# Gated mix of attention and SwiGLU: three instead of five of every eight score tiles are split between VectorE and ScalarE, in another order of scores, steps and late exponentials

## The chip, the core and the metric

The kernel runs on one core of a Trainium2 chip. A core has a matrix engine (TensorE, PE in the profile, with its weight loads on a row of their own, PEld), VectorE (DVE), ScalarE (ACT), GpSimd (POOL) and SyncE (SP), which issues the DMAs. The engines run side by side, each works through its own instructions in order, and they wait for one another by semaphores. Matrix products land in PSUM, a small memory of banks that hold 128x512 float32 values each; everything else lies in SBUF. The metric is the device time of one execution in microseconds (us), as the median of several.

## The reference

The input `x` has 2048 rows of 512. Attention with 32 heads of width 16 that share one key and one value head, a SwiGLU layer with an inner width of 1792, and a sigmoid gate per row that mixes the two:

```python
q = (x @ wq).reshape(B, S, H, Dh).transpose(0, 2, 1, 3)
k, v = x @ wk, x @ wv
scores = jnp.einsum("bhqd,bkd->bhqk", q, k) * (Dh ** -0.5)
o = jnp.einsum("bhqk,bkd->bhqd", softmax(scores), v)
a = o.transpose(0, 2, 1, 3).reshape(B, S, H * Dh) @ wo
b = (silu(x @ w_gate) * (x @ w_up)) @ w_down
g = sigmoid((x * gate_w).sum(-1, keepdims=True))
return g * a + (1 - g) * b
```

## The kernel before

**The units of attention.** Work is cut into units u = 16 h + kt: head h and one of 16 key tiles of 128 keys. A unit has two score tiles, each for 128 keys and 1024 queries. `score` (line 658) fills one score tile `pss` with two matmuls, one for each PSUM bank of 512 queries; there are only two such tiles (`ps_s`, two buffers of two banks), so a score can start only when the score before the last has been read out of PSUM. An exponential (`exps`, line 666) goes to `pt` in SBUF. `mix` (line 678) multiplies the unit's `pt` with the values into `po`. The softmax is not shifted by a maximum; a flag asks at the end whether that was safe.

**Two ways to empty a score tile.** A whole tile (kind "A") is read by one ScalarE instruction over 1024 columns. A split tile (kind "H") is read by two engines side by side: VectorE copies columns 512 to 1023 to `pt` as they are (line 662), ScalarE takes the exponential of columns 0 to 511 from PSUM ("d" in the table `EXPS`), and later, in place in SBUF, that of the copied half ("s", a late exponential). A split tile is out of PSUM sooner and costs VectorE a copy.

**The steps of the feed-forward layer.** Its products (gate, up, down) and the query projections are jobs of 12 or 15 steps. Every step is done in two halves of 64 rows: one job does its lower half while an earlier job does its upper half, so a step is a pair of matmuls at line 175 on different rows of PE. A job has a PSUM tile `pf` (three buffers), which VectorE empties: a copy for gate (line 265), a product with silu for up (line 292, or 294), a scaled sum for down (lines 327 and 329). A finished job gives its `pf` free only when that has run. The silu needs a tanh on ScalarE (line 274) and a VectorE instruction on two SBUF operands (line 282); the result is then cast and split (lines 106 and 107). GpSimd splits the weights (lines 106 and 107 on POOL).

**The block.** The order in the long stage is written out by hand. From unit 32 on, a block of four units has eight scores, 16 steps and the `mix` of four units. The table `STEPS` says in which order scores (S) and steps (F) are issued to PE, `KINDS` which score tiles are split, and `EXPS` in which order ScalarE does the exponentials: "3d" is the one that frees tile 3, "2s" the late one of tile 2. An entry is issued as soon as its score has been issued; those behind "|" come after all scores and after the tanh instructions that wait in `ACTS`. The scores run two units ahead: block k issues the scores of units 4k+2 to 4k+5 and mixes units 4k to 4k+3, so the first two units mixed have their `pt` from the block before. There are 118 full blocks of this kind. Behind the scores, VectorE gets up to 3.2 (`BUDGET`) of work that was put off: two entries of `LATER` (the division by the softmax sum, lines 687, 690, 696), then `DEFER` (silu, cast). When a job ends on a step that is followed within two steps by the score of a split tile, its evacuation is held back behind that score's copy (`HOLD`). The copy of a finished head's `po` (line 695) is issued once a number of scores of the block have been issued.

Of the kernel before, what the change touches and what calls it, by code (L numbers as in the profile page):

```python
# [50 lines left out]
STOP = 2  # L51
EARLY = 6
OUTS = (1, 2, 3, 0)
STEPS = "SSFFFFSFFSFFSFFFSFFFSFFS"
KINDS = "HHHAHHAA"
EXPS = ("0d", "1d", "0s", "2d", "3d", "4d", "1s", "5d", "6d", "7d", "2s", "|", "4s", "5s")
TURN = "SS" + "SFF" * 8
BUDGET = 3.2
AHEAD = 6
# [3 lines left out]
def tile_gated_mix(ctx, tc, x, wq, wk, wv, wo, w_gate, w_up, w_down, gate_w, out):  # L63
# [60 lines left out]
    def run(queue, n):  # L124
        for _ in range(min(n, len(queue))):
            queue.pop(0)()
# [508 lines left out]
    with tc.tile_pool(name="bpool", bufs=2) as bp:  # L635
# [15 lines left out]
        def score(u, j, half=False):  # L651
            h, kt = divmod(u, NT)
            if j == 0:
                new_pt(u)
            ps = ps_s.tile([P, 2 * CH], F32, name="pss")
            for b in range(2):
                rows = slice(b * RT, (b + 1) * RT)
                nc.tensor.matmul(ps[:, b * CH:(b + 1) * CH], ks[rows, kt * P:(kt + 1) * P], QS[h][rows, j, :],  # L658
                                 start=True, stop=True)
            halves.clock += 1  # L660
            pt = PT[u][:, j * 2 * CH:(j + 1) * 2 * CH]
            other = nc.vector.tensor_copy(pt[:, CH:], ps[:, CH:]) if half else None  # L662
            return pt, ps, other

        def exps(pt, ps, other=None, w=slice(None)):
            ins = nc.scalar.activation(pt[:, w], ps[:, w], AF.Exp, scale=SCALE)  # L666
            if other is not None:
                tc.declare_no_dep(getattr(ins, "ins", ins), getattr(other, "ins", other), reason="another bank")

        def mix(u):  # L670
            h, kt = divmod(u, NT)
            pt = PT.pop(u)
            if kt == 0:
                run(COPY, 1)
                PO[:] = [ps_o.tile([P, CH], F32, name="po")]
            po = PO[0]
            for c in range(NCH):
                nc.tensor.matmul(po[c * 2 * DH:(c + 1) * 2 * DH, :], vaug[:, kt, :], pt[:, c * CH:(c + 1) * CH],  # L678
                                 start=(kt == 0), stop=(kt == NT - 1))
            if kt == NT - 1:  # L680

                osb = hp.tile([P, CH], F32, name="osb")
                rsb = hp.tile([P, CH], F32, name="rsb", bufs=1)

                def invert(i):
                    w = slice(i * P, (i + 1) * P)
                    nc.vector.reciprocal(rsb[:, w], rsb[:, w])  # L687

                def store():
                    nc.vector.tensor_tensor(osb, osb, rsb, ALU.mult)  # L690
                    for c in range(NCH):
                        nc.sync.dma_start(o_d[h * DH:(h + 1) * DH, c * CH:(c + 1) * CH],
                                          osb[c * 2 * DH:c * 2 * DH + DH, :])

                COPY.append(lambda: nc.vector.tensor_copy(osb, po))
                LATER.extend([(0.8, lambda: nc.vector.stream_shuffle(rsb, osb, [DH] * 2 * DH))] +
                             [(1.0, lambda i=i: invert(i)) for i in range(TC)] + [(0.8, store)])
# [5 lines left out]
        def feed(k, more=True):  # L703
            for _ in range(k):
                if JOBS and more or halves.busy():
                    halves.step(more)

        def block(k, first, last, steps, kinds, order):
            more = k < NB - STOP
            tiles = [(u, j) for u in range(first, last) for j in range(2)]  # L710
            order = list(order)
            made = []

            def emit():
                while order and order[0] != "|" and int(order[0][0]) < len(made):
                    i, how = int(order[0][0]), order.pop(0)[1]
                    pt, ps, other = made[i]
                    if how == "s":
                        exps(pt, pt, w=slice(CH, None))
                    else:  # L720
                        exps(pt, ps, other, slice(0, CH) if kinds[i] == "H" else slice(None))

            for i, what in enumerate(steps):
                if what == "F":
                    if "S" in steps[i + 1:i + 3] and kinds[len(made):len(made) + 1] == "H":
                        HOLD.append(i)
                    feed(1, more)
                    HOLD.clear()
                elif len(made) < len(tiles):
                    made.append(score(*tiles[len(made)], kinds[len(made)] == "H"))  # L730
                    emit()
                    run(EVAC, len(EVAC))
                if len(made) > 3:
                    run(COPY, 1)
            if order:
                order.pop(0)
            run(ACTS, len(ACTS))
            emit()
            assert not order and len(made) == len(tiles)
            left = BUDGET  # L740
            for queue, n in ((LATER, 2), (DEFER, len(DEFER))):
                while n and queue and queue[0][0] <= left:
                    cost, f = queue.pop(0)
                    left, n = left - cost, n - 1
                    f()
            for u in range(BLOCK * k, BLOCK * (k + 1)):
                mix(u)
            halves.clock += 2 * LONG
# [7 lines left out]
        with tc.manual_schedule():  # L756
# [25 lines left out]
            for k in range(2 * BEGIN // BLOCK, NB):  # L782
                u = BLOCK * k
                if k == 2 * BEGIN // BLOCK:
                    n = u + 6 - (u + 1)
                    block(k, u + 1, u + 6, TURN, "A" * 2 * n, [f"{i}d" for i in range(2 * n)])
                elif k == NB - 1:
                    block(k, u + 2, u + 4, STEPS, "AAAA", ("0d", "1d", "2d", "3d", "|"))
                else:
                    block(k, u + 2, u + 6, STEPS, KINDS, EXPS)  # L790
                h = u // NT
                if k % (NT // BLOCK) == 0 and 0 < h < H - 1:
                    load_head(h + 1)
                if k == NB - EARLY:
                    load_o(OUTS[0], range(KD - 1))
# [119 lines left out]
```

## Time and profile before

| | us |
|---|---|
| median of 3 runs | 1374.03 (1373.33 to 1375.18) |
| the profiled execution's own time | 1375.01 |
| its span from first to last instruction | 1373.2 |
| PE busy in the span | 1344.7 |
| ScalarE busy | 1082.0 |
| VectorE busy | 866.1 |
| GpSimd busy | 391.1 |
| mean granted TensorE clock | 0.996 of full |

The span is cut by stage: until about 130 us come projections and a first stage of attention in which all tiles are whole, from about 140 to 1290 us the 118 blocks, and behind them the rest of the down products and the output projection. A row of a timeline has the start, the duration, the engine, the line, the operation, what is written and read, how many of a kind in sequence were merged (x4), and in brackets how long the engine was idle before and who ended that. Matmul durations overlap: on PE the distance from one start to the next is what counts.

### The profile page before, as it was taken

The numbers are of one execution on the slowest core, as the hardware profiler recorded it, in microseconds if no ns is written. First come the engines' busy times: TensorE is split into PE (matmuls) and PEld (weight loads), VectorE is DVE, ScalarE is ACT, GpSimd is POOL, SyncE is SP. The second block draws the span as 40 slices with busy tenths as digits, with TensorE's granted clock in tenths as the row PEclk, the third lists the DMA queues.
The fourth block names the chain that finished last, engine by engine and source line by source line (L and its number), as shares of the span: only waits on it lengthen the run. The fifth ranks groups of instructions, "written<-read, shape, count | busy, mean of one in ns | idle before, by whom it ended". The sixth has DMA issues, their size and how long they took to land. (4 is left out here: it accounts for less than half of the span.)

```text
span 1373.2 us, 27579 instructions
## 1 busy us (share of the span) xinstructions
PE 1344.7 (98%) x10755; PEld 798.9 (58%) x10755; DVE 866.1 (63%) x1458; ACT 1082.0 (79%) x1699; POOL 391.1 (28%) x408
## 2 busy tenths in 40 slices
PE   9999999999999999999999999999999999999998
PEld 7654565565655555655555565556555555655576
DVE  5554677577666666666576676667576676666532
ACT  4578898888888888888888888888888888888500
POOL 5140321052131242132131241232131331233344
PEclk9999999999999999999999999999999999999999
DMA  7455311131241231121241230131221221222154
GB/s 271 139 177 188 88 35 36 29 100 43 55 123 44 74 82 35 47 74 44 58 120 43 66 92 26 47 89 36 59 68 33 89 66 35 62 68 58 36 165 140
DMA packets 101495, 107.84 MB, mean 79 GB/s; under 512 B 9968, under 2 KB 69616, under 8 KB 99696
## 3 DMA queue, kind: packets, MB, share of 16 engines
q1 hardware_dynamic: 99632, 105.81, 26.8%
q8 instruction: 89, 1.46, 0.5%
q10 hardware_dynamic: 1728, 0.20, 0.1%
q14 instruction: 46, 0.38, 0.1%
HBM read 76.09 MB, written 29.36 MB: 77 GB/s over the span
## 5 line engine op out<-in xcount | busy, mean ns | idle before, releaser
L666 ACT ACTIVATE pt<-pss 128x512 f32<-128x512 f32 (+1 forms) x1024 | 753.9, 778 | 185.2 <-PE pss L658 166.5
L662 DVE COPY pt<-pss 128x512 f32<-128x512 f32 x590 | 395.4, 688 | 312.2 <-PE pss L658 295.9
L678 PE MATMUL po<-pt,vaug 128*32 128x512 f32 x4096 | 469.3, 597 | 0.0
L658 PE MATMUL pss<-qs,ks 64*128 64x512 f32 x2048 | 432.7, 418 | 5.9 <-DVE pt L662 4.0
L666 ACT ACTIVATE pt<-pt 128x512 f32<-128x512 f32 x590 | 351.8, 630 | 1.4 <-DVE pt L662 1.3
L658 PEld LDWEIGHTS pss<-qs,ks 64*128 64x128 f32 x2048 | 202.6, 184 | 197.4 <-issue 106.0
L678 PEld LDWEIGHTS po<-pt,vaug 128*32 128x32 f32 x4096 | 119.5, 110 | 272.1 <-issue 272.1
L175 PE MATMUL pf<-xh,wgh 64*128 64x512 f32 (+1 forms) x444 | 167.5, 394 | 5.0 <-DVE ht L292 4.4
L175 PE MATMUL pf<-xh,wuh 64*128 64x512 f32 (+1 forms) x440 | 167.2, 393 | 2.9 <-DVE sign L401 0.7
L175 PE MATMUL pf<-xl,wgh 64*128 64x512 f32 (+1 forms) x444 | 169.7, 390 | 0.0
L175 PE MATMUL pf<-xh,wgl 64*128 64x512 f32 (+1 forms) x444 | 169.3, 395 | 0.0
L175 PE MATMUL pf<-xh,wul 64*128 64x512 f32 (+1 forms) x440 | 167.2, 394 | 0.0
L175 PE MATMUL pf<-xl,wuh 64*128 64x512 f32 (+1 forms) x440 | 163.0, 390 | 0.0
L175 PE MATMUL pf<-wdl,hh 64*128 64x512 f32 (+1 forms) x427 | 158.2, 392 | 2.4 <-POOL wdl L107 2.4
L175 PE MATMUL pf<-wdh,hh 64*128 64x512 f32 (+1 forms) x427 | 157.5, 394 | 2.9 <-DVE ht L292 2.4
L106 POOL CAST wgh<-wraw 128x512 fp32r<-128x512 f32 x56 | 35.5, 633 | 432.3 <-PE pf L175 338.8
L175 PE MATMUL pf<-wdh,hl 64*128 64x512 f32 (+1 forms) x427 | 156.9, 392 | 0.0
L687 DVE RECIPROCAL rsb<-rsb 128x128 f32<-128x128 f32 x128 | 116.9, 934 | 3.1 <-issue 1.1
L106 POOL CAST wuh<-wraw 128x512 fp32r<-128x512 f32 x56 | 35.7, 638 | 259.8 <-PE pf L175 223.6
L175 PEld LDWEIGHTS pf<-xh,wgh 64*128 64x128 f32 (+1 forms) x444 | 81.2, 185 | 16.4 <-issue 6.4
L175 PEld LDWEIGHTS pf<-xh,wuh 64*128 64x128 f32 (+1 forms) x440 | 80.9, 184 | 12.8 <-issue 7.2
L175 PEld LDWEIGHTS pf<-wdh,hh 64*128 64x128 f32 (+1 forms) x427 | 79.0, 186 | 12.7 <-DVE ht L292 4.5
(157 smaller groups left out, 1590.7 us busy)
## 6 DMA issues: line engine op xcount, KB each, us to landing
wraw<-in_B_w_gate_dram SPq DMA_DIRECT2D x56, 256.0 KB
wraw<-in_B_w_up_dram SPq DMA_DIRECT2D x56, 256.0 KB
wraw<-in_B_w_down_dram SPq DMA_DIRECT2D x56, 256.0 KB
qs<-q_d SPq DMA_DIRECT2D x62, 192.0 KB
q_d<-hl SPq DMA_DIRECT2D x18, 256.0 KB
q_d<-hh SPq DMA_DIRECT2D x18, 256.0 KB
o_d<-osb SPq DMA_DIRECT2D x128, 32.0 KB
a_d<-acc SPq DMA_DIRECT2D x4, 1024.0 KB
```

The source lines that it names most:

```text
L106: eng_hi.tensor_copy(hi, src)
L175: ins = nc.tensor.matmul(self.ps, a, b, start=(i == 0 and not half), stop=(last and half != 0))
L658: nc.tensor.matmul(ps[:, b * CH:(b + 1) * CH], ks[rows, kt * P:(kt + 1) * P], QS[h][rows, j, :], start=True, stop=True)
L662: other = nc.vector.tensor_copy(pt[:, CH:], ps[:, CH:]) if half else None
L666: ins = nc.scalar.activation(pt[:, w], ps[:, w], AF.Exp, scale=SCALE)
L678: nc.tensor.matmul(po[c * 2 * DH:(c + 1) * 2 * DH, :], vaug[:, kt, :], pt[:, c * CH:(c + 1) * CH], start=(kt == 0), stop=(kt == NT - 1))
L687: nc.vector.reciprocal(rsb[:, w], rsb[:, w])
```

## The change

Three tables and one number:

```diff
-STEPS = "SSFFFFSFFSFFSFFFSFFFSFFS"
-KINDS = "HHHAHHAA"
-EXPS = ("0d", "1d", "0s", "2d", "3d", "4d", "1s", "5d", "6d", "7d", "2s", "|", "4s", "5s")
+STEPS = "SSFFFFFSFSFFFSFFSFFFFFSS"
+KINDS = "AHHAHAAA"
+EXPS = ("0d", "1d", "2d", "3d", "4d", "5d", "1s", "4s", "2s", "6d", "7d", "|")
...
-                if len(made) > 3:
+                if len(made) > 4:
                     run(COPY, 1)
```

In a block of the kernel before, tiles 0, 1, 2, 4 and 5 are split, and 3, 6 and 7 are whole. Now tiles 1, 2 and 4 are split, and 0, 3, 5, 6 and 7 are whole: two copies less on VectorE, and in place of two half exponentials twice one whole. PE still has eight scores, 16 steps and one mix in a block, in another order. The late exponentials of tiles 1, 4 and 2 stand together between 5d and 6d, and none is left behind "|", so that the tanh comes last. The copy of a head's `po` comes after the fifth score, not the fourth.

ScalarE, one block (between two others, without a tanh in it). Each row is an exponential; `pt<-pss` with 128x512 is the half of a split tile, with 128x1024 a whole tile, and `pt<-pt` a late one. Before:

```order
L666 ACTIVATE pt_4846<-pss_4847 128x512
L666 ACTIVATE pt_4846<-pss_4852 128x512
L666 ACTIVATE pt_4846<-pt_4846 128x512
L666 ACTIVATE pt_4868<-pss_4869 128x512
L666 ACTIVATE pt_4868<-pss_4878 128x1024
L666 ACTIVATE pt_4886<-pss_4887 128x512
L666 ACTIVATE pt_4846<-pt_4846 128x512
L666 ACTIVATE pt_4886<-pss_4909 128x512
L666 ACTIVATE pt_4921<-pss_4922 128x1024
L666 ACTIVATE pt_4921<-pss_4931 128x1024
L666 ACTIVATE pt_4868<-pt_4868 128x512
L666 ACTIVATE pt_4886<-pt_4886 128x512 x2
```

Now:

```order
L666 ACTIVATE pt_5269<-pss_5270 128x1024
L666 ACTIVATE pt_5269<-pss_5274 128x512
L666 ACTIVATE pt_5290<-pss_5291 128x512
L666 ACTIVATE pt_5290<-pss_5299 128x1024
L666 ACTIVATE pt_5309<-pss_5310 128x512
L666 ACTIVATE pt_5309<-pss_5319 128x1024
L666 ACTIVATE pt_5269<-pt_5269 128x512
L666 ACTIVATE pt_5309<-pt_5309 128x512
L666 ACTIVATE pt_5290<-pt_5290 128x512
L666 ACTIVATE pt_5350<-pss_5351 128x1024
L666 ACTIVATE pt_5350<-pss_5355 128x1024
```

The block opens with a whole tile, no late exponential stands among the first six, and three of them stand ahead of the last two whole tiles.

PE, from a block's first two scores to its third. Before (eight matmuls, four steps of down jobs):

```order
L658 MATMUL pss<-qs,ks 128x512 x4
L175 MATMUL pf<-wdl,hh 128x512
L175 MATMUL pf<-wdh,hl 128x512 x2
L175 MATMUL pf<-wdh,hh 128x512 x2
L175 MATMUL pf<-wdl,hh 128x512 x2
L175 MATMUL pf<-wdh,hl 128x512
L658 MATMUL pss<-qs,ks 128x512 x2
```

Now ten matmuls, five steps:

```order
L658 MATMUL pss<-qs,ks 128x512 x4
L175 MATMUL pf<-wdh,hl 128x512
L175 MATMUL pf<-wdl,hh 128x512
L175 MATMUL pf<-wdh,hh 128x512
L175 MATMUL pf<-wdh,hl 128x512
L175 MATMUL pf<-wdl,hh 128x512
L175 MATMUL pf<-wdh,hh 128x512
L175 MATMUL pf<-wdh,hl 128x512
L175 MATMUL pf<-wdl,hh 128x512
L175 MATMUL pf<-wdh,hh 128x512
L175 MATMUL pf<-wdh,hl 128x512
L658 MATMUL pss<-qs,ks 128x512 x2
```

The third score stands one step later, the fourth follows after one step instead of two, and the last two scores now stand side by side ahead of the mix.

VectorE, a block in which an up job ends before its silu has run, so that silu and product stand among the copies (the MEMSET is a marker that the lower half of a job has ended). Before:

```order
L662 COPY pt_7363<-pss_7364 128x512
L662 COPY pt_7363<-pss_7369 128x512
L662 COPY pt_7383<-pss_7384 128x512
L282 SCALAR_TENSOR_TENSOR ht_7307<-ht_7307,hs_7305 128x512
L292 TENSOR_TENSOR ht_7307<-ht_7307,pf_7175 128x512
L662 COPY pt_7411<-pss_7412 128x512
L401 MEMSET sign_84 1x1
L662 COPY pt_7411<-pss_7425 128x512
```

Now, in such a block:

```order
L662 COPY pt_9375<-pss_9380 128x512
L401 MEMSET sign_84 1x1
L662 COPY pt_9397<-pss_9398 128x512
L662 COPY pt_9415<-pss_9416 128x512
L282 SCALAR_TENSOR_TENSOR ht_9328<-ht_9328,hs_9326 128x512
L292 TENSOR_TENSOR ht_9328<-ht_9328,pf_9207 128x512
L401 MEMSET sign_84 1x1
```

Two copies stood behind the silu and its product; none stands there now. A silu directly followed by its product stands at 14 places before and at 13 now. The program still has 1024 score tiles; the copies go from 590 to 354.

## The prediction

> **What bounds the kernel now.** I read the page's head first, then the busy times of the long stage, then the timeline of single blocks, and last the waits of PE.
>
> ```profile
> span 1373.2 us, 27579 instructions
> PE 1344.7 (98%) x10755; PEld 798.9 (58%) x10755; DVE 866.1 (63%) x1458; ACT 1082.0 (79%) x1699; POOL 391.1 (28%) x408
> ```
>
> ```profile
> 200.00:1200.00 1000.00, 987.69 (x8258) 572.97 (x8256) 663.06 (x1122) 863.47 (x1392) 262.17 (x271) 1.00 0.23 61
> ```
>
> The second fence is the stretch from 200 to 1200 us: PE 988 of 1000, VectorE 663, ScalarE 863, the clock full. PE is the bound, but "busy" hides waits of less than a matmul's modelled length, so I measure blocks. These are the starts of the first and the last mix in that stretch, and the group that says how many matmuls of the mix lie in it:
>
> ```profile
> 204.94 3.64 PE L678 MATMUL po<-pt,vaug 128*32 128x512 f32 x32
> ...
> 1191.44 3.64 PE L678 MATMUL po<-pt,vaug 128*32 128x512 f32 x32
> ```
>
> ```profile
> L678 PE MATMUL po<-pt,vaug 128*32 128x512 f32 x3296 | 375.0, 595 | 0.0
> ```
>
> 3296 matmuls at 32 a block are 103 mixes, so 102 blocks took 986.5 us: 9.67 us each. An undisturbed block looks like this on PE:
>
> ```profile
> 815.52 3.64 PE L678 MATMUL po<-pt,vaug 128*32 128x512 f32 x32
> 819.09 0.74 PE L658 MATMUL pss<-qs,ks 64*128 64x512 f32 x4
> 819.66 0.39 PE L175 MATMUL pf<-xh,wgl 64*128 64x512 f32 x1
> ...
> 820.12 0.39 PE L175 MATMUL pf<-xl,wgh 64*128 64x512 f32 x1
> ...
> 820.35 0.39 PE L175 MATMUL pf<-xh,wgl 64*128 64x512 f32 x1
> ...
> 820.57 0.49 PE L658 MATMUL pss<-qs,ks 64*128 64x512 f32 x2
> 820.87 0.38 PE L175 MATMUL pf<-xh,wuh 64*128 64x512 f32 x1
> ...
> 821.33 0.43 PE L658 MATMUL pss<-qs,ks 64*128 64x512 f32 x2
> ...
> 822.00 0.48 PE L658 MATMUL pss<-qs,ks 64*128 64x512 f32 x2
> ...
> 822.94 0.47 PE L658 MATMUL pss<-qs,ks 64*128 64x512 f32 x2
> ...
> 824.61 0.43 PE L658 MATMUL pss<-qs,ks 64*128 64x512 f32 x2
> 824.97 3.64 PE L678 MATMUL po<-pt,vaug 128*32 128x512 f32 x32
> ```
>
> It takes 9.45 us: 3.57 from mix to first score, 5.88 for scores and steps. A step or a score costs 0.23 (820.12 to 820.35), the first two scores together 0.57 (819.09 to 819.66), and a score that had to wait for its tile 0.30 up to the next step (820.57 to 820.87). The mean of 9.67 is 0.22 above this block; over 118 blocks that is 26 us, about all that an easier VectorE or GpSimd could give back. Who made PE wait, from 160 to 1285 us, first on PE, then on its weight loads:
>
> ```profile
> PE pf L175 <- DVE ht L292: 6.8, 8, 1.6
> PE pss L658 <- DVE pt L662: 4.0, 7, 1.6
> PE pf L175 <- DVE acc L329: 1.0, 3, 0.4
> PE pf L175 <- DVE hs L265: 1.0, 4, 0.4
> ```
>
> ```profile
> PEld pss L658 <- ACT pt L666: 38.6, 171, 2.0
> ...
> PEld pf L175 <- DVE ht L292: 4.5, 6, 1.8
> ...
> PEld pf L175 <- DVE hs L265: 1.2, 2, 0.7
> ```
>
> VectorE's six rows are 18.5 us. The 38.6 us of weight loads that waited for an exponential are mostly their head start on the matmul and can't be added to the span; they say that a score's tile comes free only just in time, 171 times. The chain that ended last reaches back only to the output projection at 1359 us, so it says nothing of this stage.
>
> **The change part by part.** The sum is made against the profiled execution: 1375.01 us, 1.8 more than its span and 1.0 above the median of 1374.03; I carry its difference over to the median. PE's matmuls, the DMAs and GpSimd's work stay the same in number and kind, so PE's own time costs nothing either way; only waits move. Prices:
>
> ```profile
> L666 ACT ACTIVATE pt<-pss 128x1024 f32<-128x1024 f32 x434 | 426.6, 1025 | 62.8 <-PE pss L658 44.8 <-issue 8.6
> L662 DVE COPY pt<-pss 128x512 f32<-128x512 f32 x590 | 395.4, 688 | 312.2 <-PE pss L658 295.9 <-PE pf L175 3.2 <-ACT pt L666 0.5
> L666 ACT ACTIVATE pt<-pt 128x512 f32<-128x512 f32 x590 | 351.8, 630 | 1.4 <-DVE pt L662 1.3
> L666 ACT ACTIVATE pt<-pss 128x512 f32<-128x512 f32 x590 | 339.7, 597 | 122.4 <-PE pss L658 121.7
> ```
>
> ```profile
> 819.68 1.09 ACT L666 ACTIVATE pt<-pss 128x512 f32<-128x512 f32 x2 [0.69 <-PE pss L658]
> ...
> 826.26 1.67 ACT L666 ACTIVATE pt<-pt 128x512 f32<-128x512 f32 x3
> ...
> 805.58 1.94 ACT L666 ACTIVATE pt<-pss 128x1024 f32<-128x1024 f32 x2 [1.05 <-PE pss L658]
> ```
>
> *ScalarE's sum.* Instructions overlap at their ends: in a row of equals the next starts after 0.49 (1.09 less 0.597) for a half from PSUM, 0.52 ((1.67 less 0.63) / 2) for a late one, 0.92 (1.94 less 1.02) for a whole tile. Two tiles that go from split to whole save 2 x (0.49 + 0.52 - 0.92) = 0.18 us a block. That is worth nothing: ScalarE has some 7.8 us of work in 9.45, and what hides it is PE's own order.
>
> *The release of whole tiles* is what it pays. A split tile is out after about 0.69 of reading, a whole one after 1.02. How the whole tile 3 ran in the block above, and the weights of the score that took its place:
>
> ```profile
> 821.79 1.03 ACT L666 ACTIVATE pt<-pss 128x1024 f32<-128x1024 f32 x1
> ```
>
> ```profile
> 822.87 0.19 PEld L658 LDWEIGHTS pss<-qs,ks 64*128 64x128 f32 x2
> ```
>
> Score 821.33, exponential 0.46 later, end at 822.82, weights at 822.87, score at 822.94: 1.61 in all, and 0.12 from end to score. PE has seven slots of 0.23 = 1.61 between those two scores: just met. Now I walk a block of the new order, from its first score as 0. First step 0.57; after five steps PE is ready for the third score at 1.72; tile 0, now whole, is read from 0.59 (819.68 less 819.09) to 1.61 and gives 1.73. That score waited, so: next step 2.03, fourth score 2.26, and fifth after three steps 3.18. ScalarE does 0d at 0.59, 1d at 1.51, 2d at 2.25 to 2.3 (0.53 or so after its score) and 3d at 2.8; that ends at 3.82 and gives the sixth score at 3.94, where PE was ready at 3.87: 0.07 late, and 0.05 more as a score that waited. Five steps later the seventh score stands at 5.4, the eighth at 5.62; tile 5, whole, is read from 4.45 to 5.47 and gives 5.59, no wait. The mix follows 0.36 later (824.61 to 824.97): 5.98 where the old order has 5.88. Allowing 0.02 for two slots at which margins are below 0.03, I take +0.12 a block, 14.2 us in 118 blocks. Bounds: 0.04 (only one score late, and only by the 0.05; 4.7 us) and 0.25 (both late by 0.1 and their step after; 29.5 us). I take the value nearest to the walk.
>
> *The copies.* 236 of 590 go, 0.69 us each, 163 us of VectorE that lie beside PE. Their return is in the six rows: of the 4.0 in which a score waited for a copy I take three quarters, 3.0, since tiles 0 and 5 have none now and tile 2's is no longer third in a queue of three; of the other 14.5, in which a step waited for a `pf` that VectorE had not emptied, the share of copies that go, 236/590 = 0.4: 5.8. Together 8.8, bounds 0 and 18.5. Most of what remains looks like this, VectorE with GpSimd and then PE:
>
> ```profile
> 531.36 1.66 DVE L282 SCALAR_TENSOR_TENSOR ht<-ht,hs 128x512 f32<-128x512 f32 x1
> 533.12 0.69 DVE L292 TENSOR_TENSOR ht<-ht,pf 128x512 f32<-128x512 f32 x1
> ```
>
> ```profile
> 531.18 1.29 POOL L107 TENSOR_TENSOR wul<-wraw,wuh 128x512 fp32r<-128x512 f32 x1
> ```
>
> ```profile
> 534.55 0.51 PE L658 MATMUL pss<-qs,ks 64*128 64x512 f32 x2 [1.59 <-DVE pt L662]
> ```
>
> ```profile
> L282 DVE SCALAR_TENSOR_TENSOR ht<-ht,hs x52: 679/692/1822, 129.9 to 1305.9; 128x512 f32<-128x512 f32 x52
> ```
>
> A silu that takes 0.69 takes 1.66 here, until GpSimd's split of weights is over, and tile 5's copy stood behind it; the copy goes, the silu stays (13 such places for 14). The Trainium skill ("SBUF — State Buffer", section "SBUF: two separate sides") says that a VectorE instruction with two SBUF inputs and a GpSimd instruction that reads SBUF lock each other out for a whole instruction; the trace agrees, 1.66 against 0.69, and by that rule copies out of PSUM are no part of it, so the long silus stay. Were they the copies' doing, the 14.5 us on `pf` would go whole, and the sum would be 1374 + 14.2 - 17.5, about 1371.
>
> *Late exponentials, tanh.* Late ones of tiles 1, 4, 2 run from 5.4 to 6.9 of the walk; the mix needs tile 1 at 5.98 + 1.8 and tile 2 at 5.98 + 2.7: hidden. 6d and 7d then end at 7.9 and 8.9, the next block's first scores stand at 9.55 and 9.9: hidden by the mix. The tanh ends about 9.4, 1.3 later than before relative to the mix, and the silu behind it on VectorE at 10.1, ahead of the first copy at 10.4 (in that queue wait the copies, evacuations and markers of the next block):
>
> ```profile
> DVE ht L282 <- ACT ht L274: 40.8, 29, 3.4
> ```
>
> Those 40.8 us will grow and cost PE nothing, unless the silu is one of the long ones: a third of 51, each up to 0.2 late for the fourth score, 3 us at most; I take 0. The `po` copy one score later: it stands ahead of an up job's product at 4 places, 4 x 0.68 = 2.7 us at most, cover elsewhere the three `pf` buffers; 0.
>
> **Sum:** +14.2 - 8.8 = +5.4: 1380.4 against the profiled 1375.01, 1379.4 against the median.
>
> **The rivals.** *Faster:* whole tiles come free in time and VectorE's relief is full. For it: the walk's margins are hundredths, and the 0.22 a block of disturbance is larger than my 0.12; a step that waits for VectorE also gives ScalarE time, so that the two waits hide in one another. Against: the long silus. Time 1374 + 4.7 - 14 to 18.5, about 1362; it decides if the two late scores together cost less than 8.8/118 = 0.075 us a block. *Same:* the two cancel, or the copies' waits were never PE's and whole tiles fit: 1374. *Clearly slower:* no return from VectorE and the chain at 14.2 to 29.5: 1388 to 1403. For it: ScalarE is the busier of the two helpers (863 against 663) and now frees five tiles alone. The Trainium skill ("Perfetto Trace Analysis", section "Optimizing Scalar/DVE Operations") says that where these engines aren't saturated but cause bubbles, breaking instructions up may let work finish sooner; the change joins them up, and by that alone the time would be 1374 + 14.2, about 1388.
>
> **How the numbers follow.** A measurement of this kernel can tell 0.2%, 2.7 us. Chances: slower by my sum 0.40, clearly slower 0.13, same 0.14, faster 0.33. The predicted time is the first's, 1379 (its own range 1377 to 1388). The range takes in faster and most of clearly slower: 1362 to 1396.
>
> **What would show it.** Copies 354 at 0.69; blocks at about 9.7; in an undisturbed block sixth scores some 0.07 late with PE weight loads waiting on whole exponentials, 5.98 from first score to mix; the wait of line 292 on PE below 11 us in both views but not gone; the silu's wait for tanh up. I am wrong if undisturbed blocks have 5.9 or less, or if the rows of VectorE fall to nothing.

## The result and the profile after

The changed kernel takes 1366.99 us (median of 5, 1366.42 to 1368.16) against 1373.76 of the kernel before (5 runs): a ratio of 0.9953 with a 95% interval of 0.9939 to 0.9968. In a second set of runs it was 0.9970 (0.9958 to 0.9982; the run a0_after below). So it is faster by 0.3 to 0.5%, 3 to 7 us. The forecast was 1379 with 0.53 on slower and 0.33 on faster: the time lies in the range, on the other side of no change.

The page of the profiled execution, which took 1366.99 itself; the last line is the group of VectorE's copies:

```profile
span 1364.9 us, 26750 instructions
...
PE 1332.3 (98%) x10755; PEld 767.4 (56%) x10755; DVE 722.6 (53%) x1222; ACT 1061.2 (78%) x1463; POOL 390.6 (29%) x408
...
L662 DVE COPY pt<-pss 128x512 f32<-128x512 f32 x354 | 244.6, 692 | 372.4 <-PE pss L658 332.8
```

There are 354 copies for 590, at the same 0.69 us; VectorE has 144 us less to do and the kernel gains 3 to 7. Not all of the larger figure is the change's. The spans of the two profiled executions, 1373.2 and 1364.9, differ by 8.3 us; some 5 of them lie in the blocks. Another 1.7 lie in one mix of the kernel before, in which the granted clock was at half (PE's row, then that stretch with the clock as the last but two of its numbers):

```profile
1212.74 5.31 PE L678 MATMUL po<-pt,vaug 128*32 128x512 f32 x32
```

```profile
1212.74:1216.15 3.41, 3.41 (x18) 0.79 (x20) 0.49 (x1) 2.58 (x4) 0.00 (x0) 0.50 0.13 28
```

And 1.5 lie ahead of the blocks, whose first score stands at 142.37 before and at 140.90 now; from 11.25 to 14.66 the clock was at 0.50 there too. The mean clock of these two was 0.996 and 0.999, and 0.999 or 1.000 in all five runs of the changed kernel. Over the runs of the kernel before that stand beside the experiments, the time goes loosely with it: 1374.2 to 1375.7 in the five at 0.995, 1369.9 to 1373.5 in the twelve at 0.998. In the second set both kernels ran at 0.995 to 1.000 on one chip; its 3.4 us (1369.31 for 1372.69) are the fairer figure.

The stretch from 200 to 1200 us (time, then busy time and instructions of PE, its weight loads, VectorE, ScalarE and GpSimd, then the granted clock), and in it the first and the last mix on PE and the group of all of its matmuls:

```profile
200.00:1200.00 1000.00, 984.08 (x8285) 548.31 (x8281) 540.10 (x917) 847.98 (x1188) 260.44 (x270) 1.00 0.22 61
```

```profile
203.09 3.64 PE L678 MATMUL po<-pt,vaug 128*32 128x512 f32 x32
...
1196.54 3.64 PE L678 MATMUL po<-pt,vaug 128*32 128x512 f32 x32
```

```profile
L678 PE MATMUL po<-pt,vaug 128*32 128x512 f32 x3328 | 378.6, 595 | 0.0
```

3328 matmuls are 104 mixes, so 103 blocks took 993.45 us: 9.645 each, where it was 9.67. The gain is 0.03 us a block, so I look at one undisturbed block. On PE, from one mix to the next:

```profile
802.36 3.64 PE L678 MATMUL po<-pt,vaug 128*32 128x512 f32 x32
805.93 0.73 PE L658 MATMUL pss<-qs,ks 64*128 64x512 f32 x4
...
807.64 0.41 PE L658 MATMUL pss<-qs,ks 64*128 64x512 f32 x2
807.88 0.40 PE L175 MATMUL pf<-xh,wul 64*128 64x512 f32 x1
...
808.12 0.41 PE L658 MATMUL pss<-qs,ks 64*128 64x512 f32 x2
...
809.07 0.40 PE L658 MATMUL pss<-qs,ks 64*128 64x512 f32 x2
...
809.76 0.39 PE L658 MATMUL pss<-qs,ks 64*128 64x512 f32 x2
...
811.15 0.63 PE L658 MATMUL pss<-qs,ks 64*128 64x512 f32 x4
811.71 3.64 PE L678 MATMUL po<-pt,vaug 128*32 128x512 f32 x32
```

ScalarE in that block, at tile 0 (first row) and from tile 2 on (second row; the next exponential, of tile 3, starts with its end overlapped, some 0.5 later):

```profile
806.47 1.03 ACT L666 ACTIVATE pt<-pss 128x1024 f32<-128x1024 f32 x1 [0.70 <-PE pss L658]
```

```profile
808.08 1.52 ACT L666 ACTIVATE pt<-pss 128x512 f32<-128x512 f32 x2
```

And the weight loads of the third score and of the sixth, which take over tiles 0's and 3's place; behind them that of the third score in the undisturbed block of the kernel before:

```profile
807.55 0.19 PEld L658 LDWEIGHTS pss<-qs,ks 64*128 64x128 f32 x2 [0.17 <-ACT pt L666]
...
809.65 0.19 PEld L658 LDWEIGHTS pss<-qs,ks 64*128 64x128 f32 x2 [0.16 <-ACT pt L666]
```

```profile
820.53 0.22 PEld L658 LDWEIGHTS pss<-qs,ks 64*128 64x128 f32 x2 [0.21 <-ACT pt L666]
```

From the first score as 0: third score 1.71, fourth 2.19, fifth 3.14, sixth 3.83, mix 5.78. The forecast's walk had 1.73, 2.26, 3.18, 3.94 and 5.98. Whole tile 0 is read from 0.54 to 1.57; its place is loaded again 0.05 later, and PE comes to the third score at 1.71 by its own pace. No slot is lost anywhere: from the second score to the last, steps and scores stand 0.23 to 0.25 apart. In the kernel before the third score also started by PE's pace (1.48), but 0.04 after its held-back weight load, and its next step came 0.30 later; here it is 0.09 after the load, and the next step 0.24 later.

Who made PE wait, from 160 to 1280 us: on PE, then on its weight loads, then the largest wait of VectorE for ScalarE:

```profile
PE pf L175 <- DVE sign L401: 16.1, 22, 1.8
PE pss L658 <- DVE sign L401: 0.6, 1, 0.6
...
PE pf L175 <- DVE ht L292: 0.3, 1, 0.3
```

```profile
PEld pss L658 <- ACT pt L666: 110.6, 429, 1.0
```

```profile
DVE ht L282 <- ACT ht L274: 74.6, 34, 4.3
```

No score waits for a copy any more (4.0 us before), and the steps wait for a marker of 0.06 us (line 401) instead of the product of line 292. The marker isn't slow: it stands behind other work on VectorE. The weight loads wait on exponentials 429 times for 171, in this block only within their head start on the matmul.

These totals can't be set against those of before, because the same pause is put down to another row. So I measured every block on PE: the distance from the first score to the mix, over the 5.78 of the block above, and whether one slot in it was over 0.17 us late ("short") or over 0.7 ("long"). 114 blocks of each kernel, worked out from the starts on PE's timeline; sums in us over all blocks:

| | mean | quiet blocks: mean | short: number, sum | long: number, sum | all over 5.78 |
|---|---|---|---|---|---|
| before | 6.12 | 67: 5.87 | 40, 20.9 | 7, 11.9 | 38.7 |
| after | 6.08 | 75: 5.83 | 30, 15.6 | 9, 15.0 | 34.1 |
| after, again (a0_after) | 6.10 | 75: 5.83 | 30, 15.7 | 9, 17.1 | 36.3 |

A quiet block is 0.04 shorter, which is some 5 us over 118 blocks. The sums are split by kind of block: quiet blocks give some 2 us (67 x 0.09 = 6.0 before, 75 x 0.05 = 3.8 now, with more of them now), short stalls give 5.3, long ones take 3 to 5 back. What a long stall is shows the block whose first score is at 815.28. VectorE, GpSimd and PE:

```profile
816.07 0.69 DVE L662 COPY pt<-pss 128x512 f32<-128x512 f32 x1 [2.02 <-PE pss L658]
...
818.97 0.69 DVE L662 COPY pt<-pss 128x512 f32<-128x512 f32 x1 [0.81 <-ACT pt L666]
819.58 1.38 DVE L282 SCALAR_TENSOR_TENSOR ht<-ht,hs 128x512 f32<-128x512 f32 x1
820.99 0.69 DVE L292 TENSOR_TENSOR ht<-ht,pf 128x512 f32<-128x512 f32 x1
821.62 0.06 DVE L401 MEMSET sign<- 1x1 f32 x1
```

```profile
819.11 1.29 POOL L107 TENSOR_TENSOR wul<-wraw,wuh 128x512 fp32r<-128x512 f32 x1
```

```profile
821.73 0.49 PE L175 MATMUL pf<-wdh,hh 64*128 64x512 f32 x1 [1.47 <-DVE sign L401]
```

The up job's evacuation was held back behind tile 4's copy, and the silu of that job had not run yet: copy, silu (1.38 instead of 0.69 beside GpSimd's subtraction), product and marker stand in one row, and PE waits 1.47. VectorE had stood idle for 2.02 us ahead of the block's first copy, but the silu wasn't issued there: at the end of the block before, the two parts of a division and a cast came first in the queue (1.0, 0.8 and 1.2 by the program's costs), and of the 3.2 of `BUDGET` 0.2 was left for its 0.7. I call that a left-over silu; there are 13 after and 14 before. Eight of the nine long stalls after lie in blocks with one.

### The profile page after: what moved, and what is told of

The parts are those of the page before. It is cut to its first block, busy times and chain, and to the rows that moved or that the text cites. A ratio compares the mean times of both kernels' runs of the same rounds, so it can differ in the third digit from the quotient of the medians.

```text
span 1364.9 us, 26750 instructions
## 1 busy us (share of the span) xinstructions
PE 1332.3 (98%) x10755; PEld 767.4 (56%) x10755; DVE 722.6 (53%) x1222; ACT 1061.2 (78%) x1463; POOL 390.6 (29%) x408
## 5 line engine op out<-in xcount | busy, mean ns | idle before, releaser
L666 ACT ACTIVATE pt<-pss 128x1024 f32<-128x1024 f32 (+1 forms) x1024 | 841.1, 875 | 200.7 <-PE pss L658 170.4
L662 DVE COPY pt<-pss 128x512 f32<-128x512 f32 x354 | 244.6, 692 | 372.4 <-PE pss L658 332.8
L658 PE MATMUL pss<-qs,ks 64*128 64x512 f32 x2048 | 397.2, 415 | 2.0 <-ACT pt L666 1.1
L658 PEld LDWEIGHTS pss<-qs,ks 64*128 64x128 f32 x2048 | 192.4, 184 | 215.4 <-ACT pt L666 133.7
L666 ACT ACTIVATE pt<-pt 128x512 f32<-128x512 f32 x354 | 195.7, 620 | 0.0
L175 PE MATMUL pf<-xh,wuh 64*128 64x512 f32 (+1 forms) x440 | 163.6, 393 | 4.0 <-DVE sign L401 3.2
L175 PE MATMUL pf<-xh,wgl 64*128 64x512 f32 (+1 forms) x444 | 165.5, 394 | 0.0
L175 PE MATMUL pf<-xl,wgh 64*128 64x512 f32 (+1 forms) x444 | 165.4, 390 | 0.0
L175 PE MATMUL pf<-xh,wul 64*128 64x512 f32 (+1 forms) x440 | 163.8, 394 | 0.0
L175 PE MATMUL pf<-wdl,hh 64*128 64x512 f32 (+1 forms) x427 | 153.5, 391 | 2.5 <-POOL wdl L107 2.5
L175 PEld LDWEIGHTS pf<-wdh,hh 64*128 64x128 f32 (+1 forms) x427 | 78.4, 185 | 15.7 <-DVE sign L401 7.5
```

The lines of the kernel that those rows point to most:

```text
L175: ins = nc.tensor.matmul(self.ps, a, b, start=(i == 0 and not half), stop=(last and half != 0))
```

## The experiments

After the result my theory was that the change is worth what it is only as a whole: the new order gives a whole tile the time that it needs, and the whole tiles take the copies away that the new order would wait for. The rivals put the gain to the order or to the tables alone. A second question was what keeps the gain so small: left-over silus, held-back evacuations, or neither. In the expectations, C is the theory that only both parts together gain; D, that left-over silus make the long stalls, and F, that the kernel before has the same fault; E, that a whole tile needs seven slots of PE; G, that evacuations held back behind tile 4's copy make the short ones. Every ratio is to runs of the kernel before on the same chip.

**Tables alone (e1_tables), order alone (e2_steps), copy rule undone (e3_copyrule).**

```diff
# e1_tables: before, with
-KINDS = "HHHAHHAA"
-EXPS = ("0d", "1d", "0s", "2d", "3d", "4d", "1s", "5d", "6d", "7d", "2s", "|", "4s", "5s")
+KINDS = "AHHAHAAA"
+EXPS = ("0d", "1d", "2d", "3d", "4d", "5d", "1s", "4s", "2s", "6d", "7d", "|")
# e2_steps: before, with
-STEPS = "SSFFFFSFFSFFSFFFSFFFSFFS"
+STEPS = "SSFFFFFSFSFFFSFFSFFFFFSS"
# e3_copyrule: after, with
-                if len(made) > 4:
+                if len(made) > 3:
```

> The kernel before with the new tables of split tiles and of late exponentials alone (354 copies); the old order of scores and steps. Theory A (the copies gated the release of score tiles and the evacuations, and that alone made the gain of 6.8 us): 1367, within 2. Theory B (the order of scores and steps made it, since it gives every whole tile seven slots of PE): no gain, 1374 within 2. Theory C (only both together, since whole tiles on the old order come late): above 1375.

> The kernel before with the new order of scores and steps alone; five split tiles and the old late exponentials (590 copies). Theory A: 1374 within 2. Theory B: 1367 within 2. Theory C: above 1374.

> The changed kernel with the copy of a head's po issued after the fourth score again, not the fifth. All theories: 1367 within 1.5, it is a small edit; if the rule itself carries part of the gain: 1369 to 1372.

Measured: e1_tables 1383.05 us, 1.0079 (1.0063 to 1.0095), 10 us slower; e2_steps 1373.47, 1.0009 (0.9998 to 1.0019), no change; e3_copyrule 1368.85, 0.9974 (0.9962 to 0.9987), not to be told from the changed kernel's 0.9953 and 0.9970. The loss that C expected of e2_steps didn't come. In e1_tables the third score stands six slots after the first, as in the kernel before, but its tile is whole. PE there:

```profile
617.46 0.74 PE L658 MATMUL pss<-qs,ks 64*128 64x512 f32 x4
...
619.08 0.50 PE L658 MATMUL pss<-qs,ks 64*128 64x512 f32 x2
619.42 0.39 PE L175 MATMUL pf<-xh,wgh 64*128 64x512 f32 x1
```

The third score starts 1.62 after the first instead of 1.48, and the step after it 0.34 later instead of 0.30: quiet blocks take 6.05 for 5.87. That is the cost that the forecast charged to the change; it is there where the whole tile is put into the old order, and the new order takes it away. In e2_steps quiet blocks are as short as after (5.83), but 51 blocks have a short stall (22.2 us) for 40 (20.9). Which slots are late tells the parts of the change apart. I sum by how much a slot starts late against the median of the same slot in its kernel, where that is over 0.1 us, in the 110 to 113 blocks of each trace in which every slot is recorded:

| | quiet block | late scores, us | late steps, us |
|---|---|---|---|
| before | 5.87 | 7.3 | 18.3 |
| tables alone (e1_tables) | 6.05 | 0.1 | 15.5 |
| order alone (e2_steps) | 5.83 | 5.5 | 29.4 |
| after, and again (a0_after) | 5.83 | 1.3, 1.9 | 26.0, 27.4 |

Fewer copies rid the scores of their waits in either order and the steps of 2 to 3 us; the new order makes quiet blocks shorter but costs 11 us in late steps. In the changed kernel most of these wait for evacuations that the order holds back: e10_hold below takes 20 of the 27 us away.

Order 0, tables +10, both together -3 to -7: the two parts need each other. That the copy rule is worth anything isn't shown.

**One slot less for the whole tile (e9_third_early), and the changed kernel again (a0_after).**

```diff
# e9_third_early: after, with
-STEPS = "SSFFFFFSFSFFFSFFSFFFFFSS"
+STEPS = "SSFFFFSFFSFFFSFFSFFFFFSS"
```

> The changed kernel with the third score one step earlier, six slots after the first instead of seven, the rest as it is. Theory E (a whole tile is free 1.6 us after its score, seven slots of PE hide that and six do not): the third score stands at 1.62 instead of 1.48, all after it 0.13 late, 1378 to 1386. Rival (the slots do not matter, the gain came from the copies and from the last two scores side by side): 1365 to 1370.

> The changed kernel once more, on the chip of the next three: 1367 within 2 by every theory.

Measured: e9_third_early 1386.03 us, 1.0093 (1.0074 to 1.0112); a0_after 1369.31 us, 0.9970 (0.9958 to 0.9982). One step moved from before the third score to behind it costs 16.7 us. PE in e9_third_early:

```profile
809.08 0.73 PE L658 MATMUL pss<-qs,ks 64*128 64x512 f32 x4
...
810.71 0.50 PE L658 MATMUL pss<-qs,ks 64*128 64x512 f32 x2
811.05 0.39 PE L175 MATMUL pf<-xh,wgh 64*128 64x512 f32 x1
```

The weights of that third score:

```profile
810.71 0.18 PEld L658 LDWEIGHTS pss<-qs,ks 64*128 64x128 f32 x2 [0.40 <-ACT pt L666]
```

The third score is at 1.63, where its slot was 1.48, and 0.34 pass up to the next step. Quiet blocks take 6.03 for 5.83, and all blocks together 52.7 us over 5.78 for 36.3: 16.4 us, which is the difference in time. So a whole tile needs 1.6 us from its score to the score that takes its place; seven slots of 0.23 cover it, six don't, and the order of the changed kernel gives seven to tiles 0 and 3.

**The left-over silus: a larger budget after (e4_budget) and before (e5_before_budget).** 4.0 lets the silu run behind division and cast.

```diff
-BUDGET = 3.2
+BUDGET = 4.0
```

> The changed kernel with a budget of 4.0 instead of 3.2 for the put-off VectorE work behind a block, so that a silu no longer stays over for the next block (13 places in the program before, 0 then). Theory D (the nine blocks of 7.1 to 8.0 us are silus that were left over, with the marker of the next job queued behind them, 1.7 us each above an undisturbed block): 1353 to 1358. Rival (VectorE's queue is late there whatever the silu does, or the work now ahead of the copies delays those): 1365 to 1370.

> The kernel before with a budget of 4.0 instead of 3.2. Theory F (left-over silus cost the kernel before as much as the changed one; the change did nothing about them): 1373 less about 12, 1359 to 1363. Rival (before, VectorE has five copies a block and no room for the silu, so the work put ahead delays the copies): 1368 to 1376.

Measured: e4_budget 1354.10 us, 0.9863 (0.9845 to 0.9881); e5_before_budget 1359.09, 0.9895 (0.9876 to 0.9914). No silu is left over in either. Long stalls fall from 9 to 2 after and from 7 to 0 before. PE's waits of e4_budget, from 160 to 1260 us:

```profile
PE pss L658 <- DVE sign L401: 2.7, 3, 1.4
PE pf L175 <- DVE sign L401: 2.4, 8, 0.4
```

What is left there are fourth scores that come late (six, 4.0 us): a silu and a cast that waited for the tanh stand on VectorE ahead of tile 1's copy. Both kernels have the fault of the left-over silus, and one number is worth 12 to 15 us in either, two to four times the change under study.

**No evacuation held back (e10_hold).** In the changed kernel the tiles 2 and 4 hold back evacuations behind their copies; here only tile 2 does, the block's third score. (The expectation also names tile 1; no step stands right ahead of its score, so nothing is held back there.)

```diff
-                    if "S" in steps[i + 1:i + 3] and kinds[len(made):len(made) + 1] == "H":
+                    if "S" in steps[i + 1:i + 3] and len(made) == 2 and kinds[2] == "H":
```

> The changed kernel with evacuations held back behind the copy of tile 2 alone, not behind those of tiles 1 and 4. Theory G (the 15 blocks in which a step waits for a pf between 4.9 and 5.2 us after the first score, 0.55 us each, are evacuations held behind tile 4's copy, which has 0.8 us to spare): 1358 to 1362. Rival (they wait for something else, or the copies then come late): 1366 to 1370.

Measured: 1348.09 us, 0.9815 (0.9795 to 0.9835): 21 us below a0_after on the same chip and 10 below the range of G. Short stalls fall from 30 to 16 (6.8 us), long ones from 9 to 2, and late steps from 27.4 us to 7.2. VectorE of one block in the changed kernel, and what PE waits for there:

```profile
614.29 0.69 DVE L662 COPY pt<-pss 128x512 f32<-128x512 f32 x1 [0.78 <-ACT pt L666]
614.90 0.68 DVE L265 COPY hs<-pf 128x512 f32<-128x512 f32 x1
...
615.52 0.06 DVE L401 MEMSET sign<- 1x1 f32 x1
```

```profile
615.73 0.46 PE L175 MATMUL pf<-xh,wuh 64*128 64x512 f32 x1 [0.40 <-DVE sign L401]
```

The same block in e10_hold:

```profile
608.60 0.69 DVE L265 COPY hs<-pf 128x512 f32<-128x512 f32 x1 [0.22 <-PE pf L175]
609.21 0.68 DVE L662 COPY pt<-pss 128x512 f32<-128x512 f32 x1
```

With the hold, VectorE stands idle for 0.78 until tile 4 may be copied, with an evacuation behind it that could have run; `pf` comes free 1.2 us later than in e10_hold (measured from the fifth score, which starts at 613.76 and 608.63), and PE pays 0.40. Without the hold the evacuation fills the gap, and the copy starts 0.58 behind its score instead of 0.53. That the long stalls fell too was not foreseen: the silu that belongs to the evacuation now runs in that gap. VectorE of e10_hold in the block of the long stall above, ahead of tile 4's copy at 809.10:

```profile
807.71 0.68 DVE L282 SCALAR_TENSOR_TENSOR ht<-ht,hs 128x512 f32<-128x512 f32 x1
808.50 0.69 DVE L292 TENSOR_TENSOR ht<-ht,pf 128x512 f32<-128x512 f32 x1
```

**Both (e11_both, e12_before_both).** The budget of 4.0 and the narrow hold, in the changed kernel and in the one before.

> The changed kernel with both: a budget of 4.0, and evacuations held back behind tile 2's copy alone. Blocks with long stalls were 9 with 17 us in all, those with a step late near 5.1 us were 15 with 9. If the two edits remove different stalls: 1343 to 1346. If they overlap, since holding less alone took the long stalls from nine to two already: 1346 to 1349, about as with the hold alone.

> The kernel before with the same two edits. Theory H (both edits take away faults that the two kernels share, and what is left of the change is its own worth): 1348 to 1354, that is 4 to 8 above the changed kernel with both. Rival (in the kernel before, tile 5's copy has too little room behind an evacuation, so that its score comes late and the hold was needed): 1356 to 1362.

Measured: e11_both 1344.53 us, 0.9805 (0.9789 to 0.9822); e12_before_both 1355.12, 0.9881 (0.9864 to 0.9897). The two edits overlap almost wholly in the changed kernel, since either takes most long stalls away: e11_both lies in the range for edits that remove different stalls, but its ratio of 0.9805 isn't to be told from e10_hold's 0.9815. e11_both is the best version that ran, 2% below the kernel before and some 1.5 to 1.7% below the changed one (21 to 23 us, with the changed kernel at 0.9953 to 0.9970 of the 1371.64 of these runs). e12_before_both lies between its two ranges. The rival there was a late score behind tile 5's copy, the block's eighth; none is late. What is late is the fifth score (13 times, 3.6 us), for which tile 2's copy must be done, the third in a block, and the step behind the fourth (11 times, 2.1 us).

Between the two the change itself is worth 10.6 us, more than the 3 to 7 with both faults in place and than the 4 to 8 of H. Some 9 of them are in the blocks: quiet blocks take 5.83 for 5.87, short stalls are 10 (4.2 us) for 27 (12.5), and two long stalls (2.8 us) stay in e11_both, for none. Late steps are now 2.0 us against 3.3, where they had been 26 to 27 against 18. So what the new order lost by held-back evacuations and left-over silus had hidden a good part of the change's worth.

**Tile 0 split again in the new order (e7_tile0).**

```diff
# after, with
-KINDS = "AHHAHAAA"
-EXPS = ("0d", "1d", "2d", "3d", "4d", "5d", "1s", "4s", "2s", "6d", "7d", "|")
+KINDS = "HHHAHAAA"
+EXPS = ("0d", "1d", "2d", "3d", "4d", "5d", "0s", "1s", "4s", "2s", "6d", "7d", "|")
```

> The changed kernel with tile 0 split again (four of eight, 472 copies, its late exponential ahead of the others). If a copy more at the head of a block makes evacuations push tile 2's copy back, as before the change: 14 blocks with the fifth score 0.35 late, 1371 to 1376. If a copy at that place has room: 1367 to 1370.

Measured: 1386.80 us, 1.0103 (1.0087 to 1.0120), outside both expectations; both theories fall. A split tile was to be out of its place sooner. ScalarE, VectorE and PE at the head of a block:

```profile
532.80 0.63 ACT L274 ACTIVATE ht<-hs 128x512 f32<-128x512 f32 x1
```

```profile
533.46 0.69 DVE L282 SCALAR_TENSOR_TENSOR ht<-ht,hs 128x512 f32<-128x512 f32 x1 [2.63 <-ACT ht L274]
534.07 1.28 DVE L662 COPY pt<-pss 128x512 f32<-128x512 f32 x2
```

```profile
533.07 0.73 PE L658 MATMUL pss<-qs,ks 64*128 64x512 f32 x4
...
534.90 0.50 PE L658 MATMUL pss<-qs,ks 64*128 64x512 f32 x2
```

The tanh comes last on ScalarE and ends at the next block's first scores. VectorE stands at the silu for it, and tile 0's copy stands behind the silu: it starts at 1.00 of the block, and the third score at 1.83 instead of 1.71. Quiet blocks rise to 5.94 and long stalls to 13 (20.7 us). A whole tile 0 has no copy that could be queued there; tile 1's, the first one, is needed two slots later, for the fourth score. That is why the late tanh costs the changed kernel so little. e7_tile0 also has one late exponential more ahead of the tanh; how much of the loss is the copy's alone isn't shown.

**GpSimd without its subtraction (e13_pool).** The weights' low parts are made by a second cast, not by a subtraction, so the feed-forward layer is computed from wrong low parts.

```diff
# after, with
-        split(hi, lo, raw, nc.gpsimd, nc.gpsimd)
+        if pool is wp:
+            nc.gpsimd.tensor_copy(hi, raw)
+            nc.gpsimd.tensor_copy(lo, raw)
+        else:
+            split(hi, lo, raw, nc.gpsimd, nc.gpsimd)
```

> The changed kernel with the weights' low parts made on GpSimd by a second cast, 0.63 us with one input, in place of a subtraction, 1.3 us with two (the feed-forward part is then computed from wrong low parts; every other instruction stays). If a silu is long because a GpSimd instruction is still running: none above 1.35 us, the long stalls shorter by about 0.5 each, 1362 to 1366. If it is long by something else: some still at 1.6 to 1.8, 1367 to 1370.

Measured: 1360.49 us, 0.9921 (0.9905 to 0.9938), some 4 to 7 us below the changed kernel and 1.5 below the lower range; late steps are 21.8 us for 26 to 27. All silus on VectorE (ns: least, median, longest), of the changed kernel and of e13_pool, where the lines stand four further down:

```profile
L282 DVE SCALAR_TENSOR_TENSOR ht<-ht,hs x51: 691/693/1709, 128.4 to 1298.0; 128x512 f32<-128x512 f32 x51
```

```profile
L286 DVE SCALAR_TENSOR_TENSOR ht<-ht,hs x51: 681/693/1029, 129.0 to 1293.7; 128x512 f32<-128x512 f32 x51
```

The longest goes from 1.71 to 1.03 us when GpSimd's instruction beside it is shorter; nothing on VectorE was changed. And of the silus of line 282 that took over 0.8 us, 64 in the traces of before, after, a0_after, e10_hold and e13_pool, each ends 0.54 to 0.55 us after the GpSimd instruction beside it (in the prediction's rows, 533.02 after 532.47). So a long silu is one that waits for a GpSimd instruction to end.

## Why the prediction was wrong

- **The release of whole tiles, +14.2 us: this step failed.** The runs showed about -5 us in its place (quiet blocks 5.83 for 5.87, 118 times; e2_steps, with the order alone, has the same 5.83). The mechanism is real: it costs 16.7 us in e9_third_early and 10 in e1_tables. But the walk found it in an order that had room for it, because three rows were carried to places that they don't fit. The lag from score to ScalarE was taken from a split tile (0.59); here it was 0.54 for tile 0 and 0.44 for tile 2. The 0.30 up to the next step was measured behind a score whose weight load had been held back to 0.04 before it; the walk charged it to a third score that was late by 0.01, where 0.24 was measured. And 3d was put at 2.8 where it came at about 2.65, so the sixth score was not late at all. Each is 0.05 to 0.15 us, and the walk's late scores were late by 0.01 and 0.07. A walk whose answer hangs on so little should have had "no score late" as a case of its own, and its lower bound of 4.7 us should have been below 0: the old order pays the 0.30 behind its third score too, and the new one loses it.
- **The copies, -8.8 us: right in size, not in its parts.** It was 3.0 for scores and 5.8 for steps. Where copies alone go, late scores lose 7.2 us and late steps 2.8 in the old order (before to e1_tables), 4 and 2 to 3 in the new one (e2_steps to after).
- **Evacuations in the new order: a term that the sum doesn't have.** It let the steps' waits fall with the copies. The order alone raises late steps from 18.3 to 29.4 us, and in the changed kernel they are 26.0 to 27.4. The long stalls are part of it: they were forecast to stay, 13 silus for 14, and did, but got longer and more (11.9 us to 15 to 17), as an evacuation held behind tile 4's copy takes silu and product with it. Quiet blocks -5, late scores -5 to -6, late steps +8 to +9 come to some -1 to -3 us, and the blocks lost 2.4 to 4.6. So that the time lies in the range is in part luck: a term that was too high by 19 us and one that is missing have opposite signs. With both faults taken out the change is worth 10.6 us.
- **The long silus as a lock, not the copies' doing: right.** The longest silu after is 1.71 us with 236 copies fewer, and 1.03 when GpSimd's subtraction goes. The Trainium skill ("SBUF — State Buffer", section "SBUF: two separate sides") gives the rule that these instructions of VectorE and GpSimd lock each other out; e13_pool bears it out.
- **Joining halves into wholes as a step back: wrong here.** By that rival the time was about 1388. The rule on breaking instructions up that stood beside it is in the Trainium skill ("Perfetto Trace Analysis", section "Optimizing Scalar/DVE Operations"). e1_tables and e9_third_early come near that (1383 and 1386); with one more slot before the tile is needed again the joined instruction cost nothing.
- **The tanh later, taken as 0: nearly right, and for less than the reason given.** The silu's wait for it rose from 40.8 to 74.6 us, and PE paid little: three fourth scores were late, 1.3 us in all. I had named the time up to the fourth score as cover; e7_tile0 shows a third score late 30 times (8.6 us) once tile 0 has a copy behind that silu.
- **Line 292 below 11 us but not gone: wrong as a sign.** It is 0.3 now, and the marker of line 401 has 16.1. It is the same queue, named by its last entry.
- **"Wrong if undisturbed blocks have 5.9 or less":** they have 5.83. The sign was the right one.

## What to carry to other kernels

Before an evacuation is made longer, set the time from one write of its buffer to the next against what the whole chain takes (here 0.54 to the start, 1.03 of reading, 0.05 to the next weights): in slots of 0.23 us seven were enough, six cost 17 us in the program. Change the order and the kind of work together, since each alone was worth nothing or less. And when the waits name an instruction of 60 ns, look at what stands ahead of it on its engine: here that was worth 21 to 23 us, three to seven times the change itself. And look at the granted clock of both runs before a gain of 0.5% is put down to a change.

## What was not expected of the hardware

- A score's start doesn't show all that its wait costs. By the medians over all blocks, the weight load started 0.23 us ahead of the third score in e2_steps, 0.09 after the change, 0.01 before it, and together with it in e1_tables and e9_third_early; the next step came 0.23, 0.25, 0.30 and 0.34 after that score. So a weight load that an exponential holds back costs PE up to a tenth of a us more than the score's own start shows. What PE does in that time, the traces don't show.
- The lag from a score's start to ScalarE's was 0.59 for a half tile before and 0.54 for a whole one after, at the first score of a block, with ScalarE idle ahead of both (medians of 118 blocks; e1_tables has 0.54 too); what makes the difference was not tried.
